# A kernel of attention and two feed-forward layers: four writes and two reads in place of one and five for the transposed coarse probabilities of the later pairs

## The chip, the core and the metric

The kernel runs on one core of a Trainium2 chip. Its five engines each work off their own instructions in order: TensorE (PE in the profile; PEld is its weight load), VectorE (DVE), ScalarE (ACT), GpSimd (POOL) and SyncE (SP), which issues nearly all transfers. The metric is the time of one execution on the device in microseconds, the median over runs.

## What is computed

Attention over 4 batches of 8 heads, 576 positions of 64 numbers, then two feed-forward layers over the 2304 tokens. The attention is the sum of a coarse one, over means of four positions, repeated to full length, and a local one, over a band of three positions to each side. Cut to that:

```python
q_d = q.reshape(B, H, Sd, factor, D).mean(axis=3)      # k_d, v_d alike; Sd = 144
out_d = sm_attn(q_d, k_d, v_d)                         # softmax(q_d k_d' / 8) v_d
out_up = np.repeat(out_d, factor, axis=2)
mask = np.abs(pos[:, None] - pos[None, :]) < factor
scores = np.where(mask, scale * np.matmul(q, k.transpose(0, 1, 3, 2)), -1000000000.0)
out_local = np.matmul(softmax(scores), v)
x = (out_up + out_local)                               # to [2304, 512]
x = _moe_ref(x, w_in, w_out)                           # h = x @ w_in; h * sigmoid(1.702 h) @ w_out
return _moe2_ref(x, w2_in, w2_out)                     # h = x @ w_in; max(0.01 h, h) @ w_out
```

## The kernel before

A pair is two heads of one batch: 16 pairs, numbered 0 to 15 in the order in which they are worked on (`Job` objects, the index into `jobs`). Pairs 0 to 7 are interleaved by a table of tokens, `ORDER`. Pairs 8 to 15, the later pairs, run beside the first feed-forward layer: its loop over blocks of tokens and slices of the hidden layer (`units`) calls `l1_part` (line 860), `gate` and `l2` (line 901), and each unit has two places in which steps of a later pair may stand (`turns`). `Job.slots` is the table of these steps: its keys are the places, counted from the pair's start, and its strings name the steps in the order in which they are issued. A new pair starts every six places.

All engines follow the order in which the program is written (a manual schedule). So on SP the transfers of a later pair stand in one line with those of the feed-forward layers: loads of weights `s` (line 168), writes of converted weights `wsf` (line 232), rows of the attention's result `xd` (line 745), and each is issued when its turn has come and its waits are over. Transfers signal on eight semaphores used in turn; one that takes a semaphore waits until the transfer eight before it has landed.

The steps of a later pair that matter here, with the names in the profile:

- `Mud` scales the coarse probabilities `pd` (128 rows of 3 x 160 numbers, line 539); `Bd` transposes them in blocks of 32 x 32 on DVE (line 588) into a second `pd` tile; `Bds` writes that to DRAM, tensor `tdd` (line 596); `Bdl` reads `tdd` back into `pdT` (line 602) so that the key positions lie on the partitions: 96 rows and 48 rows.
- `Bl` transposes the local probabilities `P` in blocks (line 662), `Bls` writes them to DRAM, tensor `td`, in four writes (line 671), `Bll` reads them back as `pT` (line 674).
- `vh` loads the values for the local attention in two transfers (line 398). `Va0`, `Va1`, `Vb0`, `Vb1` sum the values by fours on POOL (line 440).
- `Vd` multiplies `pdT` by the summed values on PE (`avd`, line 632) and `Y` multiplies `pT` by `vh` (`av_halves`, line 700), right behind it; both stand at place 13 or 14, between units of the feed-forward layer.

After the later pairs come the rest of the first layer and the second layer, to the end of the span; PE works through them in order.

Of the kernel before, what the change touches and what calls it, by code (L numbers as in the profile page):

```python
# [7 lines left out]
F32 = mybir.dt.float32  # L8
# [8 lines left out]
P = 128  # L17
# [6 lines left out]
DK = (96, 48)  # L24
# [3 lines left out]
def attn_moe_kernel(ctx: ExitStack, tc, qT_d, kT_d, vh_d, vg_d, w1a, w2a, w1b, w2b, outT):  # L28
    nc = tc.nc
# [6 lines left out]
    SD = S // FACTOR  # L36
# [56 lines left out]
    dram = ctx.enter_context(tc.tile_pool(name="dram", bufs=1, space=bass.MemoryType.DRAM))  # L93
# [11 lines left out]
    def slot(name):  # L105
# [20 lines left out]
        out=ident, in_=ident, compare_op=ALU.not_equal, fill=1.0, base=0,  # L126
# [5 lines left out]
    for r in (slice(0, KT), slice(KT, P)):  # L132
        nc.gpsimd.affine_select(
            out=bands[r], in_=bands[r], compare_op=ALU.is_ge, fill=NEG, base=0,
# [3 lines left out]
            out=bands[r], in_=bands[r], compare_op=ALU.is_ge, fill=NEG, base=2 * HALO,  # L138
# [183 lines left out]
    ND, DS, DN = 3, 40, 48  # L322
    SDP = -(-SD // 32) * 32

    class Job:
# [265 lines left out]
            )  # L591

        def blocks_d_out(self):
            self.td = dram.tile([P, SDP // 32, ND * 32], F32, name=f"tdd_{self.nm}")
            t = self.td_t.rearrange("p t n -> p (t n)").rearrange("p (c n) -> p c n", n=ND * 32)
            nc.sync.dma_start(out=self.td, in_=t)

        def blocks_d_in(self):
            self.pdT = self.tile([DK[0], 2, ND * P], "pdT")
            for c in range(SDP // 32):  # L600
                n = min(32, SD - c * 32)
                nc.sync.dma_start(
                    out=self.pdT[c % 3 * 32 : c % 3 * 32 + n, c // 3, :].rearrange("p (b n) -> p b n", b=4),
                    in_=self.td[:, c].rearrange("(b k) n -> k b n", b=4)[:n],
                )

        def avd(self, tag):
# [169 lines left out]
        def slots(self):  # L777
            names = {
                -2: "q k",
                1: "Qd",  # L780
                3: "S Kd",
                4: "A0 A1 Mx",
                5: "Sb",
                6: "Ex va vb",
                7: "Sd Mxd Exd Sm Rc Mu",
                8: "Rcd Mud Bd Bds Bl Va0 Vb0 vh Bls",
                10: "Bdl Va1 Vb1 Bll",
                14 if self is jobs[-1] else 13: "Vd Y Od X0 X1",
                16: "O",
            }  # L790
            st = self.steps()
            st.update({
                "Bd": self.blocks_d, "Bds": self.blocks_d_out, "Bdl": self.blocks_d_in,
                "Bl": self.blocks, "Bls": self.blocks_out, "Bll": self.blocks_in,
                "Y": lambda: self.av_halves("h"), "X0": lambda: self.out(0), "X1": lambda: self.out(1), "O": self.store,
            })
            return {i: [lambda n=n: self.step(st, n) for n in x.split()] for i, x in names.items()}
# [454 lines left out]
    with tc.manual_schedule(engines={ET.PE, ET.DVE, ET.Pool, ET.Activation, ET.SP}):  # L1252
# [32 lines left out]
        for u in range(UNITS, len(units)):  # L1285
# [25 lines left out]
            else:  # L1311
# [3 lines left out]
                if m in XSUM:  # L1315
                    a = XSUM.index(m) * 8 // len(XSUM)
# [61 lines left out]
```

## Time and profile before

| | us |
|---|---|
| median of 3 runs | 852.65 (852.0 to 852.66) |
| the profiled execution | 853.28 |
| its span on the core | 851.5 |
| around the span | 1.78 |
| PE busy in the span | 839.5 |
| granted TensorE clock, share of full | 0.998 |
| DMA issued by SP | 203.95 MB in 76800 packets |

The span runs from the first to the last instruction. A row of a timeline names the start in the span and the duration, the engine (SPq and PEq are the sequencers of SP and PE, where waits and issues stand), the line of the kernel, the operation, and the tiles as out<-in, with the count of instructions merged into the row; what stands in brackets is idle time before it and what ended it. A line of the kernel is L596 and so on. The duration of a transfer's row on SP is the time that its issue takes on SP, not the time until the data are there; that is the landing time.

### The profile page before, as it was taken

The page shows a single profiled execution, that of the slowest core. Times are in us where ns is not written, and L with a number is a line of the kernel's source. Part 1 is how long each engine was busy: PE and PEld are TensorE (multiplying, and loading weights), DVE is VectorE, ACT ScalarE, POOL GpSimd, SP SyncE. Part 2 cuts the span into 40 slices and gives each one's busy share as a digit, 9 for nine tenths or more (in the row PEclk, how much of TensorE's full clock was granted, in tenths as well). Part 3 has the DMA queues.
Part 4 walks back from the last instruction along what each step waited for, and adds up shares of the span by engine and source line. Part 5 has one row for each costly group of instructions (what it writes and reads, how often), then busy time and mean ns, then how long its engine had stood idle before and what let it go on. Part 6 is the DMA issues. An engine that isn't in the chain of part 4 may idle for free.

```text
span 851.5 us, 15694 instructions
## 1 busy us (share of the span) xinstructions
PE 839.5 (99%) x5736; PEld 762.6 (90%) x5736; DVE 539.5 (63%) x950; ACT 405.5 (48%) x972; POOL 475.2 (56%) x470
## 2 busy tenths in 40 slices
PE   8899999999999999999999999999999999999998
PEld 5677878887887788899999999999999999999998
DVE  6877776655567543467655757468564767573565
ACT  6876554433334332555655534455434454334460
POOL 6554433745446443777746833459554577455574
PEclk9999999999999999999999999999999999999999
DMA  9755545375765642989949978977779877787654
GB/s 292 250 161 183 183 144 157 116 238 170 196 191 144 221 132 101 341 335 420 370 150 324 343 268 277 334 248 259 265 257 353 286 235 271 267 287 266 221 190 181
DMA packets 76877, 204.95 MB, mean 241 GB/s; under 512 B 14656, under 2 KB 30016, under 8 KB 70400
## 3 DMA queue, kind: packets, MB, share of 16 engines
q1 hardware_dynamic: 76800, 203.95, 70.8%
q8 instruction: 45, 0.74, 0.4%
q14 instruction: 32, 0.26, 0.1%
HBM read 155.42 MB, written 48.50 MB: 239 GB/s over the span
## 4 chain that ended last, share of the span: by engine, by line
PE 92%; DVE 3%; ACT 1%; DMA 1%; issue 1%; SPq 1%; POOL 0%; DVEq 0%; POOLq 0%; ACTq 0%
PE h L860 23%; PE acc L901 22%; PE p L1107 21%; PE h L1032 21%; PE avd L632 1%; PE scd L549 1%; PE sc L455 1%; PE av L684 1%; DMA s<-w1a 1%; PE idle L1225 1%; ACT a L510 1%; PE av L700 0%; DMA pT<-td 0%; PE pt L651 0%; DVE s L188 0%
## 5 line engine op out<-in xcount | busy, mean ns | idle before, releaser
L1086 POOL TENSOR_TENSOR ring<-raw,ring 128x384 fp32r<-128x384 f32 x148 | 166.5, 1136 | 144.3 <-ACT ring L1084 142.8
L860 PE MATMUL h<-xh,w 128*128 128x512 f32 (+1 forms) x640 | 198.6, 373 | 0.0
L1107 PE MATMUL p<-ring,v 128*128 128x384 f32 x900 | 178.9, 334 | 0.0
L901 PE MATMUL acc<-gh,w 128*128 128x512 f32 (+1 forms) x560 | 173.2, 372 | 0.0
L1107 PEld LDWEIGHTS p<-ring,v 128*128 128x128 f32 x900 | 158.1, 188 | 0.1
L1032 PE MATMUL h<-x,v 128*128 128x384 f32 x672 | 137.4, 334 | 0.0
L860 PEld LDWEIGHTS h<-xh,w 128*128 128x128 f32 x640 | 119.1, 188 | 17.3 <-issue 1.4
L886 POOL TENSOR_TENSOR gl<-g,gh 128x512 fp32r<-128x512 f32 (+1 forms) x59 | 71.8, 1216 | 97.2 <-ACT gh L159 96.5
L1032 PEld LDWEIGHTS h<-x,v 128*128 128x128 f32 x672 | 118.4, 188 | 0.0
L860 PE MATMUL h<-xl,w 128*128 128x512 f32 (+1 forms) x320 | 117.9, 368 | 0.0
L901 PEld LDWEIGHTS acc<-gh,w 128*128 128x128 f32 x560 | 104.1, 188 | 14.8 <-issue 0.4
L901 PE MATMUL acc<-gl,w 128*128 128x512 f32 (+1 forms) x280 | 103.7, 370 | 0.0
L880 DVE SCALAR_TENSOR_TENSOR g<-g,h 128x512 f32<-128x512 f32 (+1 forms) x80 | 50.4, 630 | 79.1 <-ACT g L879 78.6
L879 ACT ACTIVATE g<-h 128x512 f32<-128x512 f32 (+1 forms) x80 | 44.0, 550 | 100.5 <-PE h L860 96.7
L1039 ACT ACTIVATE raw<-raw 128x384 f32<-128x384 f32 x72 | 37.9, 526 | 109.1 <-DVE raw L1042 108.9
L1072 DVE TENSOR_TENSOR raw<-raw,raw 128x384 f32<-128x384 f32 x84 | 76.7, 946 | 15.1 <-ACT raw L1039 13.0
L1042 DVE TENSOR_TENSOR raw<-h,u 128x384 f32<-128x384 f32 x72 | 40.1, 557 | 72.1 <-PE h L1032 71.6
L1084 ACT ACTIVATE ring<-raw 128x384 fp32r<-128x384 f32 x150 | 73.5, 515 | 0.0
L1032 PE MATMUL h<-x_ra,v 128*128 128x384 f32 x336 | 72.5, 334 | 0.0
L159 ACT ACTIVATE gh<-g 128x512 fp32r<-128x512 f32 (+1 forms) x70 | 41.7, 595 | 62.7 <-DVE g L880 58.8
L860 PEld LDWEIGHTS h<-xl,w 128*128 128x128 f32 x320 | 60.4, 189 | 6.9
L211 POOL TENSOR_TENSOR w<-t,w 128x512 fp32r<-128x512 f32 x25 | 33.1, 1327 | 48.5 <-ACT w L159 42.2
(188 smaller groups left out, 1271.3 us busy)
## 6 DMA issues: line engine op xcount, KB each, us to landing
v<-ws SPq DMA_DIRECT2D x42, 1024.0 KB, 6.5
v<-ws SPq DMA_DIRECT2D x72, 512.0 KB, 4.6
ws<-wo SPq DMA_DIRECT2D x16, 1792.0 KB, 10.3
s<-w1a SPq DMA_DIRECT2D x16, 512.0 KB, 4.6
s<-w2a SPq DMA_DIRECT2D x16, 512.0 KB, 4.6
s<-w1b SPq DMA_DIRECT2D x16, 512.0 KB, 5.8
s<-w2b SPq DMA_DIRECT2D x16, 512.0 KB, 9.4
v<-ws SPq DMA_DIRECT2D x24, 256.0 KB, 4.4
```

The lines of the kernel that those rows point to most:

```text
L159: return nc.scalar.activation(out=out, in_=in_, func=AF.Copy, scale=scale)
L860: nc.tensor.matmul(h, w[:, kc * P : (kc + 1) * P], xs[kc][part], start=kc == 0 and i == 0, stop=kc == KC - 1 and i == 2,)
L879: lambda: nc.scalar.activation(out=g, in_=h[:, :n], func=AF.Tanh, scale=0.5 * 1.702),
L880: lambda: nc.vector.scalar_tensor_tensor(out=g, in0=g, scalar=1.0, in1=h[:, :n], op0=ALU.add, op1=ALU.mult),
L886: lambda: on(G).tensor_tensor(out=gl, in0=g, in1=gh.bitcast(F32), op=ALU.subtract),
L901: nc.tensor.matmul(acc[c][:, :n], w[:, cs], g, start=m == 0 and i == 0, stop=m == NM - 1 and i == 2)
L1032: nc.tensor.matmul(h, w[:, a, ks], x, start=not more and kt == 0 and k == 0, stop=kt == 1 and k == 2, skip_group_check=True,)
L1042: nc.vector.tensor_tensor(out=out, in0=h, in1=u, op=ALU.add)
L1072: nc.vector.tensor_tensor(out=o, in0=a, in1=b, op=ALU.subtract)
L1084: nc.scalar.activation(out=hi, in_=t, func=AF.Copy)
L1086: e.tensor_tensor(out=lo, in0=t, in1=hi.bitcast(F32), op=ALU.subtract)
L1107: nc.tensor.matmul(self.bank[pair, ct][:, :N2], w[:, q, a, cs], g, start=not more and q == 0 and k == 0, stop=q == QC - 1 and k == 2, skip ...
```

## The change

Three things, for pairs 8 to 15 alone:

- the tensor `tdd` in DRAM is laid out with the key position outermost, [160, 4, 96] in place of [128, 5, 96]. It is written in four transfers of 32 partitions each, every partition as five pieces of 96 numbers (384 bytes), in place of one transfer of 128 partitions with 1920 bytes each;
- `pdT` is read in two transfers, 96 and 48 partitions with one piece of 1536 bytes each, in place of five of 32 (the last 16) partitions with four pieces of 384 bytes each;
- in the table of places `Bls` stands ahead of `Va0 Vb0 vh`, and `Bll` ahead of `Va1 Vb1`.

```diff
         def blocks_d_out(self):
-            self.td = dram.tile([P, SDP // 32, ND * 32], F32, name=f"tdd_{self.nm}")
-            t = self.td_t.rearrange("p t n -> p (t n)").rearrange("p (c n) -> p c n", n=ND * 32)
-            nc.sync.dma_start(out=self.td, in_=t)
+            self.td = dram.tile([SDP, 4, ND * 32], F32, name=f"tdd_{self.nm}")
+            td = self.td.rearrange("(c k) b n -> b k c n", k=32)
+            for b in range(4):
+                t = self.td_t[b * 32 : (b + 1) * 32].rearrange("p t n -> p (t n)")
+                nc.sync.dma_start(out=td[b], in_=t.rearrange("p (c n) -> p c n", n=ND * 32))
 
         def blocks_d_in(self):
             self.pdT = self.tile([DK[0], 2, ND * P], "pdT")
-            for c in range(SDP // 32):
-                n = min(32, SD - c * 32)
+            for kh, a in enumerate((0, DK[0])):
                 nc.sync.dma_start(
-                    out=self.pdT[c % 3 * 32 : c % 3 * 32 + n, c // 3, :].rearrange("p (b n) -> p b n", b=4),
-                    in_=self.td[:, c].rearrange("(b k) n -> k b n", b=4)[:n],
+                    out=self.pdT[: DK[kh], kh, :], in_=self.td[a : a + DK[kh]].rearrange("p b n -> p (b n)")
                 )
...
-                8: "Rcd Mud Bd Bds Bl Va0 Vb0 vh Bls",
-                10: "Bdl Va1 Vb1 Bll",
+                8: "Rcd Mud Bd Bds Bl Bls Va0 Vb0 vh",
+                10: "Bdl Bll Va1 Vb1",
```

The engines PE, DVE, ACT and POOL have the same instructions in the same order in both kernels; only SP's line differs, and the waits that PE makes. On SP, the transfers of pair 13 (the numbers in the names count tiles; 32x5x96 is partitions by pieces by numbers, x4 is four in a row):

```order
-L596 DMA tdd_1_3368<-pd_1_16_3366 128x480
-L398 DMA vh_1_18_3374<-vh 64x2x320 x2
-L671 DMA td_1_3377<-P_1_17_3370 32x2x320 x4
-L232 DMA wsf_104<-t_3_0_3144 128x512
+L598 DMA tdd_1_3368<-pd_1_16_3366 32x5x96 x4
+L671 DMA td_1_3375<-P_1_17_3373 32x2x320 x4
+L398 DMA vh_1_18_3382<-vh 64x2x320 x2
+L232 DMA wsf_104<-t_3_0_3147 128x512
 L745 DMA xd_0_93<-x_0_23_3302 128x576
-L602 DMA pdT_1_19_3440<-tdd_1_3368 32x4x96 x4
-L602 DMA pdT_1_19_3440<-tdd_1_3368 16x4x96
-L674 DMA pT_1_5_2970<-td_1_3377 128x640
+L603 DMA pdT_1_19_3443<-tdd_1_3368 96x384
+L603 DMA pdT_1_19_3443<-tdd_1_3368 48x384
+L674 DMA pT_1_5_2970<-td_1_3375 128x640
```

The writes of `tdd` are four, those of `td` have moved ahead of the loads of `vh`, and three reads of `pdT` are gone; from the first write up to the read of `pT` there are 14 transfers before and after. On PE, at the products of the same pair, the waits before (each name in brackets is one semaphore; DMAHW0 to 7 are those of the transfers):

```order
1430 L632 MATMUL avd_1_20_3535<-pdT_1_19_3440,vd_1_3_2968 64x160 [waits DMAHW4_49,DMAHW3_49,DMAHW5_49,DVE_49,Pool_49]
1431 L632 MATMUL avd_1_20_3535<-pdT_1_19_3440,vd_1_3_2968 64x160
1432 L632 MATMUL avd_1_20_3535<-pdT_1_19_3440,vd_1_3_2968 64x160 [waits DMAHW7_49,DMAHW6_49,Pool_49]
1434 L700 MATMUL avd_1_20_3535<-pT_1_5_2970,vh_1_18_3374 64x64 [waits DMAHW0_49]
1435 L700 MATMUL av_1_21_3540<-pT_1_5_2970,vh_1_18_3374 64x64
```

and now:

```order
1430 L632 MATMUL avd_1_20_3535<-pdT_1_19_3443,vd_1_3_2968 64x160 [waits DMAHW6_49,DVE_49,Pool_49]
1431 L632 MATMUL avd_1_20_3535<-pdT_1_19_3443,vd_1_3_2968 64x160
1432 L632 MATMUL avd_1_20_3535<-pdT_1_19_3443,vd_1_3_2968 64x160 [waits DMAHW7_49,Pool_49]
1434 L700 MATMUL avd_1_20_3535<-pT_1_5_2970,vh_1_18_3382 64x64 [waits DMAHW2_49,DMAHW0_49]
1435 L700 MATMUL av_1_21_3540<-pT_1_5_2970,vh_1_18_3382 64x64 [waits DMAHW3_49]
```

The products on `pdT` wait for one transfer each in place of three and two; the first two products on `pT` wait for the two loads of `vh` by name.

## Rows read from the trace of the kernel before

**Rows 1.** The page's busy times: engine, us, share of the span, instructions.

```profile
PE 839.5 (99%) x5736; PEld 762.6 (90%) x5736; DVE 539.5 (63%) x950; ACT 405.5 (48%) x972; POOL 475.2 (56%) x470
```

**Rows 2.** Who waited for whom: us in total, times, longest.

```profile
PE avd L700 <- DMA pT<-td: 1.3, 1, 1.3
PE avd L632 <- DMA pdT<-tdd: 0.7, 1, 0.7
```

**Rows 3.** Timeline of PE, pair 13: start us, us, what, [idle before].

```profile
270.65 0.39 PE L901 MATMUL acc<-gh,w 128*128 128x512 f32 x1
271.71 1.09 PE L632 MATMUL avd<-pdT,vd 96*64 96x160 f32 x8 [0.68 <-DMA pdT<-tdd]
274.11 0.27 PE L700 MATMUL avd<-pT,vh 64*64 64x64 f32 x1 [1.31 <-DMA pT<-td]
```

**Rows 4.** Timeline of SP, pair 13: start us, us, issues.

```profile
263.00 0.34 SPq L596 DMA_DIRECT2D tdd<-pd  x1
263.44 1.77 SPq L398 DMA_DIRECT2D vh<-vh  x2
265.31 1.96 SPq L671 DMA_DIRECT2D td<-P  x4
267.31 0.42 SPq L232 DMA_DIRECT2D wsf<-t  x1
267.77 0.45 SPq L745 DMA_DIRECT2D xd<-x  x1
268.27 2.43 SPq L602 DMA_DIRECT2D pdT<-tdd  x5
270.74 0.43 SPq L674 DMA_DIRECT2D pT<-td  x1
```

**Rows 5.** DMA issues by line: KB each, median us from issue to landing.

```profile
vh<-vh SPq DMA_DIRECT2D x16, 160.0 KB, 3.1
pT<-td SPq DMA_DIRECT2D x8, 320.0 KB, 3.3
tdd<-pd SPq DMA_DIRECT2D x8, 240.0 KB, 2.1
xd<-x SPq DMA_DIRECT2D x4, 32.0 KB, 2.6
```

**Rows 6.** Single source lines: ns min/median/max of an issue, first and last start.

```profile
L596 SPq DMA_DIRECT2D tdd<-pd x8: 319/336/345, 161.2 to 302.9; - x8
L671 SPq DMA_DIRECT2D td<-P x32: 303/426/937, 163.1 to 306.3; - x32
L398 SPq DMA_DIRECT2D vh<-vh x16: 597/607/1365, 161.6 to 304.0; - x16
L602 SPq DMA_DIRECT2D pdT<-tdd x40: 429/432/511, 166.0 to 309.8; - x40
```

**Rows 7.** Timeline of DVE, pair 13: the transpose that td is written from.

```profile
262.90 0.80 DVE L662 STREAM_TRANSPOSE P<-P 128x640 f32<-128x640 f32 x1
```

**Rows 8.** DMA issues of 243 to 248 us (pair 12), then of 268 to 271.

```profile
pT<-td SPq DMA_DIRECT2D x1, 320.0 KB, 3.2
pdT<-tdd SPq DMA_DIRECT2D x4, 48.0 KB, 3.5
...
pdT<-tdd SPq DMA_DIRECT2D x4, 48.0 KB, 2.3
```

**Rows 9.** Line 632: PE's separate waits, ns min/median/max.

```profile
L632 PEldq EVENT_SEMAPHORE  x36: 51/51/642, 36.3 to 313.4; - x36
```

**Rows 10.** Timeline, pairs 10 and 11: the issue of pT and PE's first product on it.

```profile
209.07 0.42 SPq L674 DMA_DIRECT2D pT<-td  x1
...
212.49 0.28 PE L700 MATMUL av<-pT,vh 64*64 64x64 f32 x2
...
228.18 0.42 SPq L674 DMA_DIRECT2D pT<-td  x1
...
232.07 0.34 PE L700 MATMUL av<-pT,vh 64*64 64x64 f32 x4
```

## The prediction

> **What bounds the kernel now.** The page's busy times come first: PE is busy for 839.5 us of a span of 851.5 us [rows 1], 99%. A change that leaves every matmul where it is can only act through the 12 us in which PE has nothing to do, and this one touches eight places of them, the two blocks of value products (lines 632 and 700) of each later pair, numbered 8 to 15 here. So the second view is the list of who waited for whom, read for PE waiting on the transfers that the change rewrites. It has one wait on pdT and one on pT, each a single time [rows 2]: seven of the eight pairs show none. The third view, PE's timeline, says where: pair 13. The last matmul of line 901 starts at 270.65, the products on pdT at 271.71 after 0.68 us of idle time, those on pT at 274.11 after 1.31 us more [rows 3]. Without the waits they would start at about 270.65 + 0.39 and go on at once, and the eight take 1.09 us with the wait between them, so the stretch from 271.04 to 274.11 holds some 2.0 to 2.7 us of stall: the most that any shortening of this path could give back, 0.3% of the time.
>
> The fourth view, SP's timeline, says why pT comes late there. SP issues one transfer after another without a pause from 263.00 to 270.74: the write of tdd, two loads of vh, four writes of td, wsf, xd, five reads of pdT, then the read of pT [rows 4]. pT is not late because its data are late; it stands in line behind 14 others. From its issue to PE's start are 274.11 - 270.74 = 3.37 us, which is the usual landing time of pT, 3.3 us [rows 5]. The step that decides is therefore **when SP's turn comes to pT**, and the change must be counted in SP's issue slots.
>
> **The change, part by part.** *Four writes for one.* Three issues are added ahead of pT. The trace has no write of 32 rows by 5 pieces; the nearest is the write of td, 32 partitions by 2 pieces from the same kind of tile: 426 ns in the median [rows 6], and four take 2.00 us with the gaps between them (265.31 to 267.31 [rows 4]), 0.50 each. The reads of pdT, which also walk 32 rows by 4 pieces of 384 bytes, take 432 ns, five in 2.47 us, 0.49 each. I take 0.49: +1.47 us. Bounds: a plain 128-row write takes 319 ns at best, a load of vh 607 ns in the median [rows 6]; over the four writes that is 4 x (0.319 - 0.426) = -0.43 and 4 x (0.607 - 0.426) = +0.72 us about the value taken.
>
> *Two reads for five.* Three issues go: 3 x 0.49 = -1.47 us. The two that stay are a row of 1536 bytes per partition and take what the read of pT takes, 0.43 [rows 4].
>
> *The loads of vh behind the writes of td.* The same six issues in another order: 0 us for pT, which stands behind both. The writes of td need the DVE transpose, done at 262.90 + 0.80 = 263.70 [rows 7]; the four writes of tdd keep SP busy until 263.00 + 0.44 + 3 x 0.49 = 264.91, so no wait appears. vh would go out at 266.9 and about 267.9, later than now by some 3.4 us, and land 3.1 us on [rows 5], by 271.0; PE wants it with pT at 274.1. Cover 3 us, and in the other pairs it is issued at least two slots before pT and lands sooner than pT does. The reads of pT and the pooling of v swap places in the text only: they are on different engines.
>
> Pair 13 anew: 263.00 + 0.44 + 1.47 (tdd) + 2.00 (td) + 1.87 (vh) + 0.46 (wsf) + 0.50 (xd) = 269.74, two reads of pdT to 270.72, pT issued at **270.72 instead of 270.74**. The sum is three more and three fewer of the same thing on the same queue: 0.0 us.
>
> *What lands later?* pdT's reads now start 1.5 us later, at 269.74 and 270.23. Their landing: 2.3 us for the narrow reads in this stretch, 3.5 where a load of 512 KB goes ahead [rows 8], 3.3 for the larger pT: 272.0 to 273.7, before pT's 274.0. PE then starts its pdT products later but still ends them before pT is there; the stall moves from one label to the other and keeps its end. Where a weight load goes ahead, the same bytes drain in the same order, and fewer pieces do not make them slower.
>
> *The queue's bytes.* Ahead of wsf and xd now stand 320 KB of td (4 x 80), then 320 KB of vh: the same load in front of pdT and pT. The 512 KB ahead of pair 12's reads put 1.2 us on pdT, and nothing on pT: 3.2 us [rows 8].
>
> *PE's own waits.* Per pair the first product on pdT waits for three things instead of five and the second for two instead of three, while the first product on pT gains a wait and its neighbour another, since vh is no longer covered by an earlier wait. A separate wait takes 51 ns [rows 9]; one less and one more is 0, with bounds of 8 x 0.051 = 0.4 us either way.
>
> *The writes' landing.* SP may issue the reads of pdT only when all four writes of tdd have landed. The last goes out at 264.4, the first read at 269.74: 5.3 us of room. The write lands in 2.1 us now, and the writes of xd with 256 bytes per row (32 KB over 128 partitions), the nearest thing to pieces of 384 bytes, in 2.6 [rows 5]. Hidden, with 2.7 us to spare.
> The Trainium skill ("DMA: Bandwidth & Descriptors", section Specifications) speaks against the change here: under 512 bytes a transfer is read, modified and written, and line rate is lost. The 0.5 us between 2.6 and 2.1 agrees in sign. By it the new writes would be the slow kind, and the sum would still be 0.0 as long as they land within the room; what comes if they do not is the second rival.
>
> **The sum.** Profiled execution 853.28 us (span 851.5 and 1.78 around it), change 0.0: 853.3. The median of the runs is 852.65, 0.63 below the profiled one, so the forecast for the median is **852.6**. A difference of under 0.2% (1.7 us) is about what a measurement of this kernel cannot tell from no change.
>
> **Rivals.** *The issue of the new writes is dearer.* If five pieces per row cost what vh's issue costs, pT goes out 0.72 us later in every pair. Pair 13 pays 0.72. Pair 10 has no slack: pT issued at 209.07 lands at 212.4, PE starts on it at 212.49 [rows 10]; it pays 0.65. Pair 11: 228.18 + 3.3 = 231.5 against 232.07, slack 0.6, pays 0.15. Together +1.5: 854.1, still within 0.2%. For it: vh's 607 ns are not explained by its count of pieces, 64 x 2, which is that of a read of pdT, 32 x 4. Against: td's writes, the closest shape, are at 426. Chance 0.10.
>
> *Slower: small writes land late.* The reads of pdT on SP then wait for tdd, and pT, q, kT and the weight loads are queued behind that wait. It decides from a landing time of 5.3 us in pair 13; at 7 us the wait is 1.7 there, up to 1.7 in pair 10 and 1.1 in pair 11: +4.5, 857.1. Against: no small write in the views is near it (2.1 and 2.6 in the median). Chance 0.06.
>
> *Faster: the stall of pair 13 goes.* The writes of td start 0.4 us sooner (264.91 against 265.31), and the two loads of vh took 1.77 us there against 2 x (0.607 + 0.05) = 1.31 by the median: one issue was stretched by 0.46. If such stretches belong to the transfer and not to the moment, pT goes out 0.5 sooner; with cheap writes 0.9. To reach 0.2% more than half the stall would have to go, by a read of pT that is also 0.8 us quicker once 576 small pieces no longer run ahead of it: 852.65 - 2.0 = 850.6. Against: 512 KB ahead of it do not move its 3.2 us. Chance 0.07.
>
> *It does nothing that can be seen,* because every move is inside one queue's line: that is the forecast, 0.77 for it.
>
> **How the numbers follow.** The range takes the bounds of the costs: below, -0.43 (cheap writes) - 0.46 (the stretch gone) - 0.4 (PE's waits) = -1.3; above, +1.5 (dear writes) + 0.3 of another stretch in pair 13 or 10 = +1.8. So 851.3 to 854.4, which leaves out most of the second and third rival, 0.13, and some of the tails. Faster by over 0.2%: 0.07; slower: 0.06 from the late landing and 0.03 from dear writes with a stretch on top, 0.09; within: 0.84.
>
> **What would show it.** In the profile after: in pair 13 SP's line runs from the first write of tdd to pT in 7.7 us, as now, with four issues of about 0.43 at its head and two before pT; PE starts on pT within 0.5 us of 274.1 on the span's clock; the list of waits still has pT as PE's one wait on a transfer of these, a little longer, and pdT's shorter or longer by what pT's changes the other way. Wrong would be: a wait of SP at line 603 (the second rival), issues of line 598 near 0.6 (the first), no wait on pT at all (the third), or a wait on vh at line 700 (then the cover of 3 us was misread).

## The result, and the profile after

The changed kernel takes **857.99 us** (854.79 to 862.09, 8 runs) against 852.65 (851.54 to 853.54, 8 runs) for the one before: 1.0063 times as long, with a 95% interval of 1.0040 to 1.0087. The forecast was 852.6, no change, with a range up to 854.4. A later comparison (2 runs of the changed kernel) gave 857.92 against 852.43, 1.0068 (1.0048 to 1.0088). So the change makes the kernel about 5.4 us slower, and the prediction of no change was wrong: the time lies 3.6 us above the upper end of its range.

The profiled execution took 860.19 us, its span is 858.4. The page's busy times answer [rows 1]:

```profile
PE 841.5 (98%) x5736; PEld 763.7 (89%) x5736; DVE 538.5 (63%) x950; ACT 405.2 (47%) x972; POOL 475.7 (55%) x470
```

PE is busy 2.0 us longer with the same 5736 matmuls, and idle for 16.9 us instead of 12.0. Part of the first is chance: in this one execution the granted clock is 0.50 from 51.8 to 55.2 us, ahead of the later pairs, where it is 1.00 in the kernel before and in the second profile of the changed kernel (below). The list of waits names the idle time (us in total, times, longest; against [rows 2]):

```profile
PE avd L632 <- DMA pdT<-tdd: 5.1, 5, 3.4
PEld avd L700 <- DMA pT<-td: 0.9, 3, 0.3
```

Before, PE waited for pdT once, 0.7 us; now five times, 5.1 us. The longest is in pair 13, on PE's timeline (start, duration, [idle before]; against [rows 3]):

```profile
275.97 0.39 PE L901 MATMUL acc<-gh,w 128*128 128x512 f32 x1
279.75 0.49 PE L632 MATMUL avd<-pdT,vd 96*64 96x160 f32 x4 [3.40 <-DMA pdT<-tdd]
280.63 0.80 PE L632 MATMUL avd<-pdT,vd 48*64 48x160 f32 x4 [0.39 <-DMA pdT<-tdd]
281.27 0.36 PE L700 MATMUL avd<-pT,vh 64*64 64x64 f32 x1
```

From the last matmul of line 901 to the products on pT are 5.30 us; in [rows 3] it was 3.46. SP's timeline for the same pair, against [rows 4]:

```profile
268.66 2.53 SPq L598 DMA_DIRECT2D tdd<-pd  x4
271.29 1.82 SPq L671 DMA_DIRECT2D td<-P  x4
273.21 1.25 SPq L398 DMA_DIRECT2D vh<-vh  x2
274.51 0.59 SPq L232 DMA_DIRECT2D wsf<-t  x1
275.16 0.42 SPq L745 DMA_DIRECT2D xd<-x  x1
275.62 1.12 SPq L603 DMA_DIRECT2D pdT<-tdd  x2
276.85 0.37 SPq L674 DMA_DIRECT2D pT<-td  x1
```

The line is the one that was forecast: pT is issued at 276.85, 8.19 us behind the first write (before 7.74, forecast 7.7; one of the four writes was stretched to 1.18 us). What differs is the time from issue to landing (KB each, median us; all transfers of the stretch in which the later pairs run; against [rows 5] and the 2.3 and 3.5 us of [rows 8]):

```profile
vh<-vh SPq DMA_DIRECT2D x16, 160.0 KB, 3.0
pT<-td SPq DMA_DIRECT2D x8, 320.0 KB, 4.7
tdd<-pd SPq DMA_DIRECT2D x32, 60.0 KB, 1.8
pdT<-tdd SPq DMA_DIRECT2D x8, 144.0 KB, 4.5
pdT<-tdd SPq DMA_DIRECT2D x8, 72.0 KB, 4.3
```

The new writes land sooner than the old one, 1.8 us against 2.1, vh as before, but **pT lands in 4.7 us instead of 3.3 and pdT in about 4.4**. The transfer rates point to the reason. Two rows of the busy times by stretch, first of before, then of after, from the first write of tdd to the issue of pT in pair 13 (the last two columns are the DMA engines' busy share and GB/s):

```profile
263.00:270.70 7.70, 7.70 (x36) 6.33 (x34) 6.76 (x12) 2.77 (x5) 6.10 (x9) 1.00 0.71 207
```

```profile
268.70:276.80 8.10, 7.66 (x34) 6.01 (x32) 7.18 (x13) 3.13 (x7) 6.53 (x8) 1.00 0.55 142
```

The same 14 transfers are issued in these stretches. Before, the DMA engines move 207 x 7.7 = 1.59 MB in the time; after, 142 x 8.1 = 1.15 MB, although it is 0.4 us longer (in the second profile of the changed kernel, without a stretched write, 153 x 7.2 = 1.10 MB). SP is busy all the time, but with small transfers first: eight issues for 560 KB, and only then 1.1 MB in six issues. When pT is issued, some 0.44 MB more than before are still to be moved.

### The profile page after: what moved, and what is told of

Read it like the earlier page. It is cut to its first block, busy times and chain, and to the rows that moved or that the text cites. A ratio compares the mean times of both kernels' runs of the same rounds, so it can differ in the third digit from the quotient of the medians.

```text
span 858.4 us, 15704 instructions
## 1 busy us (share of the span) xinstructions
PE 841.5 (98%) x5736; PEld 763.7 (89%) x5736; DVE 538.5 (63%) x950; ACT 405.2 (47%) x972; POOL 475.7 (55%) x470
## 4 chain that ended last, share of the span: by engine, by line
PE 90%; DMA 5%; SPq 1%; DVE 1%; ACT 1%; issue 0%; DVEq 0%; ACTq 0%
PE h L860 22%; PE acc L901 21%; PE p L1107 20%; PE h L1032 20%; DMA pdT<-tdd 2%; DMA kT<-kT 1%; PE sc L455 1%; PE avd L632 1%; PE scd L549 1%; PE av L684 1%; DMA s<-w2a 1%; DMA a<-qT 1%; DMA a<-vg 1%; PE avd L700 0%; PE pt L651 0%
```

## Where the time went, in one table

For each of the eight pairs four moments were read off, all counted from the first write of tdd: the issue of the first bulk transfer behind tdd, td and vh (wsf, a weight load or xd, 256 to 512 KB), the issue of pT, its landing, and the length of the block, which is the time from the start of PE's last product before line 632 to that of its first after line 700. A block without a wait takes 1.58 us (pair 15: 1.74). In pair 13 before: bulk 267.31 - 263.00 = 4.31, pT issued 7.74, there 11.06, block 4.11. The table has the means over the pairs and the sum of the blocks, one profile each, and the ratio of the times. The labels are those of the experiments below.

| kernel | bulk issued | pT issued | pT there | bulk to pT there | sum of blocks | time / before |
|---|---|---|---|---|---|---|
| before | 4.06 | 7.50 | 10.77 | 6.70 | 15.4 | 1 |
| after | 5.69 | 7.71 | 12.24 | 6.55 | 20.7 | 1.0063 |
| after, again | 5.62 | 7.62 | 12.26 | 6.64 | 21.1 | 1.0068 |
| e1_layout | 5.95 | 7.89 | 12.00 | 6.04 | 17.9 | 1.0046 |
| e2_order | 4.17 | 7.69 | 11.08 | 6.91 | 15.3 | 1.0008 |
| e3_v_first | 4.21 | 6.33 | 10.49 | 6.28 | 14.6 | 0.9999 |
| e4_v_first_old | 2.91 | 6.50 | 9.83 | 6.92 | 14.2 | 0.9974 |
| e5_four_five | 5.82 | 9.02 | 12.29 | 6.46 | 21.5 | 1.0085 |
| e6_split | 5.70 | 8.96 | 12.41 | 6.70 | 20.8 | 1.0086 |
| e7_reads_early | none | 6.94 | 11.10 | | 17.6 | 1.0021 |
| e8_best | none | 5.69 | 8.92 | | 13.3 | 0.9967 |
| e9_both | none | 5.78 | 8.98 | | 13.7 | 0.9973 |

The blocks account for the loss in size: 20.7 - 15.4 = 5.3 us, and the medians differ by 857.99 - 852.65 = 5.3. That the two agree so closely is luck, since blocks come from one execution and medians from several: the spans of the two profiled executions differ by 858.4 - 851.5 = 6.9 us, and in the second profile of the changed kernel the blocks add 5.8 us and the span 4.7. Pair 13 pays 2.3 of it (4.11 to 6.42); pairs 8 to 11, which had no wait before, pay 0.3 to 1.2 each.

## The experiments

Two theories came first. **Q**: the order of SP's queue is to blame; vh's 320 KB now stand right ahead of the bulk transfers and the reads, whatever the size of the pieces. **L**: the layout is to blame; small pieces are slow to write or wide rows slow to read.

**Layout alone** (the four writes and two reads of the change, the table of places of before):

```diff
-                8: "Rcd Mud Bd Bds Bl Bls Va0 Vb0 vh",
-                10: "Bdl Bll Va1 Vb1",
+                8: "Rcd Mud Bd Bds Bl Va0 Vb0 vh Bls",
+                10: "Bdl Va1 Vb1 Bll",
```

(against the changed kernel). 

> The new layout alone (four writes of tdd, two reads of pdT), with the table of places of before, so that the loads of vh stand ahead of the writes of td. Theory Q (the queue): after the change 320 KB of vh, 256 KB of wsf and up to 288 KB of xd are issued within 2.4 us right ahead of the reads, and the reads wait in the queue behind these bytes; the pieces' size does not matter. Then, with vh early again, pT lands 3.3 to 3.9 us after its issue (median; before 3.3, changed kernel 4.7), pdT 3 to 3.8, and the time is 852 to 854.5 us. Theory L (the layout: pieces of 384 bytes written, rows of 1536 bytes read): the landings stay at 4.4 and more, and the time at 856 to 859.

Measured 855.91 against 852.48, 1.0046 (1.0027 to 1.0065): between the ranges of Q (up to 854.5) and L (from 856). So are the landings:

```profile
pT<-td SPq DMA_DIRECT2D x8, 320.0 KB, 4.1
pdT<-tdd SPq DMA_DIRECT2D x8, 144.0 KB, 3.5
pdT<-tdd SPq DMA_DIRECT2D x8, 72.0 KB, 3.3
```

**Order alone** (the layout, write and reads of before, the table of places of the change):

```diff
-                8: "Rcd Mud Bd Bds Bl Va0 Vb0 vh Bls",
-                10: "Bdl Va1 Vb1 Bll",
+                8: "Rcd Mud Bd Bds Bl Bls Va0 Vb0 vh",
+                10: "Bdl Bll Va1 Vb1",
```

> The new table of places alone (the writes of td ahead of the loads of vh), with the old layout (one write, five reads). Theory Q: vh's bytes now go out after those of td, close ahead of the reads, but the five reads of pdT give the queue 2.4 us to drain before pT is issued: pdT lands later than before (3 to 4.5 us instead of 2.8), pT in 3.3 to 4.2, the time is 853 to 856 us. Theory L: nothing moves, 852 to 853.5 us, landings as before.

Measured 853.23, 1.0008 (0.9995 to 1.0022): no difference that can be seen (the value lies in both forecasts). So most of the loss comes with the layout, and Q as stated falls. But the landings of e1_layout do not suit L either. In pair 13 pT lands in 3.4 us, about as before, and in four pairs in 4.4 to 5.3; the median is 4.1. The wide rows are those of pdT: the first read of each pair lands in 2.5 to 2.9 us in pairs 9, 10, 13 and 14, where wsf or xd goes ahead of it, and in 4.2 to 5.1 in pairs 8, 11, 12 and 15, where a weight load of 512 KB does. The narrow reads of before show the same split, 2.1 to 2.5 and 3.9 to 4.6 us. So the shape of the wide rows is not what makes them slow.

**vh ahead of everything**, with the layout of the change, then with that of before:

```diff
-                8: "Rcd Mud Bd Bds Bl Bls Va0 Vb0 vh",
+                8: "vh Rcd Mud Bd Bds Bl Bls Va0 Vb0",
```

> The changed kernel with the two loads of vh moved to the head of place 8, ahead of the steps that SP waits for, where SP stands idle before; nothing else differs. Theory Q: the 320 KB are gone from the line, pT is issued about 6.5 us after the first write of tdd instead of 8.2 and lands 3.2 to 3.9 us later; PE waits on pT or pdT at most once, by under 2 us; 850 to 852.5 us. Theory L: the landings stay at 4.4 us and more and the time stays above 854.

> The kernel of before with the loads of vh at the head of place 8 (and the writes of td right behind that of tdd); old layout, one write and five reads. Theory Q: pT is issued about 6.4 us after the write of tdd instead of 7.7, lands in 3.3 us, the stall of pair 13 shrinks by about 1.3 us: 850.5 to 852 us, the same as the new layout with vh first within 0.5 us. Theory L: as fast as that or faster, while the new layout with vh first stays slow.

Measured 851.58, 0.9999 (0.9984 to 1.0014), and 850.55, 0.9974 (0.9965 to 0.9984). The second beats the kernel before. Of the two theories' forecasts for e3_v_first, Q has the time (850 to 852.5) and L the landing (pT in 4.6 us in the median). vh out of the way gains 6.4 us on the changed kernel and 1.9 on the one before, since bulk and pT are issued 1.0 to 1.5 us sooner; what is left between the two, 1.0 us by the medians and 2.1 by the ratios, is the layout's. The table shows a later arrival: in e3_v_first pT is issued even 0.17 us sooner than in e4_v_first_old (6.33 against 6.50) and is there 0.66 us later (10.49 against 9.83), while the bulk starts 1.30 us later (4.21 against 2.91). It does not explain the time, though: pT is 0.8 to 1.5 us later in the four pairs behind a weight load, which have slack for it here, and in pair 13 no later; the blocks add 0.4 us.

That gave a third theory, **S**: what decides is when the bulk is issued. Three issues moved from behind the bulk to ahead of it put the bulk off, and pT, which must wait for the bulk's bytes, comes later by as much; the three issues saved behind the bulk give back little.

**Four writes, but five reads** (rows of 1536 bytes, 32 partitions at a time; places as before):

```diff
-            for kh, a in enumerate((0, DK[0])):
+            for c in range(SDP // 32):
+                n = min(32, SD - c * 32)
                 nc.sync.dma_start(
-                    out=self.pdT[: DK[kh], kh, :], in_=self.td[a : a + DK[kh]].rearrange("p b n -> p (b n)")
+                    out=self.pdT[c % 3 * 32 : c % 3 * 32 + n, c // 3, :],
+                    in_=self.td[c * 32 : c * 32 + n].rearrange("p b n -> p (b n)"),
```

> The new layout with four writes of 32x5x96, but read in five transfers (32 or 16 partitions, one piece of 1536 bytes each); table of places as before. Theory S (what costs is the issue slots moved ahead of the bulk transfers: whatever is added ahead of wsf, xd or the weight load makes these and then pT later, and slots saved behind them give nothing): three slots are added and none is saved, pT is issued 1.4 us later than before, about 9.2 us after the first write in pair 13, lands in 3.0 to 3.5 us after that because the five reads stand between the bulk and it; 855.5 to 857.5 us. Rival L (wide rows are slow to read, or small pieces slow to write, by themselves): pT and pdT land in 4.4 us or more as well, on top of the later issue; 858 us or more.

Measured 859.86 against 852.19, 1.0085 (1.0072 to 1.0099), 2.4 us above the upper end of what was expected. The landings are what S says (issues and landings of the stretch of the later pairs):

```profile
pT<-td SPq DMA_DIRECT2D x8, 320.0 KB, 3.2
pdT<-tdd SPq DMA_DIRECT2D x32, 48.0 KB, 3.0
```

The same wide rows, read out of the same layout, land about as fast as the narrow ones did before (3.0 us against 2.8). Yet pT is not there any sooner than in the changed kernel: 12.29 us after the first write, against 12.24. It is issued 1.3 us later and lands 1.3 us faster. Against e1_layout, from which it differs by its number of reads alone, the three reads more cost 1.13 us of issue (9.02 against 7.89) and 0.29 us of arrival (12.29 against 12.00). So three slots behind the bulk are worth a quarter of themselves in the mean. They are not worth nothing, though: in pair 13 they are worth 1.27 us (12.85 against 11.58), and the times differ by 0.4%. The mean hides a split: behind a weight load (pairs 8, 11, 12, 15) pT comes 0.1 us sooner with five reads than with two, in the other four pairs 0.7 later, and pairs 10 and 13, which have no slack, are among these.

**Four writes of the old kind**: no small pieces, no wide rows, nothing but three more issues.

```diff
-            nc.sync.dma_start(out=self.td, in_=t)
+            for b in range(4):
+                nc.sync.dma_start(out=self.td[b * 32 : (b + 1) * 32], in_=t[b * 32 : (b + 1) * 32])
```

> Layout, reads and table of places of before; only the one write of tdd is cut into four of 32 partitions, 1920 bytes each. No small piece is written, no wide row is read. Theory S: three slots are added ahead of the bulk transfers, pT goes out 1.0 to 1.4 us later; its landing stays at 3.0 to 3.5 us; 855 to 857 us. Rival L: nothing of its two causes is here, only three issue slots: pT 1.0 to 1.4 us later costs only what the slack of pairs 13, 10 and 11 does not cover, 853.5 to 855 us.

Measured 859.89, 1.0086 (1.0069 to 1.0103), again 2.9 us above S's upper end, and no different from e5_four_five with its small pieces and wide rows. **So L falls: neither small pieces nor wide rows are needed for a loss of this size; three issue slots ahead of the bulk are enough.** Here no slot is saved behind the bulk, so pT itself goes out 1.46 us later than before (8.96 against 7.50); that the loss does not need this rests on the changed kernel, where it goes out 0.2 us later, on its second profile below, and on e1_layout against e5_four_five. The landings of this kernel, and SP's timeline in pair 13:

```profile
pT<-td SPq DMA_DIRECT2D x8, 320.0 KB, 3.3
tdd<-pd SPq DMA_DIRECT2D x32, 60.0 KB, 1.7
```

```profile
266.68 2.48 SPq L597 DMA_DIRECT2D tdd<-pd  x4
...
272.61 0.42 SPq L232 DMA_DIRECT2D wsf<-t  x1
...
273.56 2.43 SPq L603 DMA_DIRECT2D pdT<-tdd  x5
276.04 0.43 SPq L675 DMA_DIRECT2D pT<-td  x1
```

wsf goes out 5.93 us after the first write instead of 4.31, and pT is there 3.16 us after its issue, at 279.20: 6.59 us after wsf. Before, that stretch was 274.06 - 267.31 = 6.75, in e5_four_five 6.61, in the changed kernel 281.23 - 274.51 = 6.72, with pT issued 3.4 us behind wsf in three of them and 2.3 in the last.

How much each side counts can be estimated from the kept traces: nine of the twelve profiles have a bulk transfer ahead of the reads, which makes 72 arrivals of pT, and a least-squares fit gives each pair a constant and each of the two delays a weight. Behind a weight load (pairs 8, 11, 12, 15) the arrival moves by 0.95 us for each us of the bulk's issue and by 0.10 for each us of pT's own. Behind wsf or xd (pairs 9, 10, 13, 14) it moves by 0.46 and 0.42, all four give or take 0.1. So S holds as it stands for the first four pairs; in the others, pair 13 with the longest stall among them, pT's own turn counts about as much as the bulk's.

Of the 2 to 3 us that S had missed, a part is the clock. In the profiles of these two kernels the granted clock is at its lower level, 1.2 of 2.4 GHz, for 6.8 us behind the stall of pair 13, twice as long as before; 3.4 us more at half speed are up to 1.7 us. The row for e6_split (PEclk is the third figure from the right):

```profile
276.90:283.70 6.80, 5.91 (x64) 4.27 (x65) 2.52 (x9) 1.31 (x8) 0.00 (x0) 0.50 0.87 253
```

**The reads ahead of the bulk**, in the layout of the change:

```diff
-                8: "Rcd Mud Bd Bds Bl Bls Va0 Vb0 vh",
-                10: "Bdl Bll Va1 Vb1",
+                8: "Rcd Mud Bd Bds Bl Bls vh Bdl Bll Va0 Vb0",
+                10: "Va1 Vb1",
```

> The changed kernel with the two reads of pdT and the read of pT at the end of place 8, right behind the loads of vh and ahead of wsf, the weight loads and xd (in pair 13: tdd x4, td x4, vh x2, pdT x2, pT, then the bulk). Theory S: nothing of the bulk is ahead of pT any more, it is issued 6.6 to 7.5 us after the first write and lands in 3 to 3.5 us, PE does not wait for it in any pair but perhaps 13; 849.5 to 852 us. Rival L: the rows and pieces are slow wherever they stand: landings of pdT and pT of 4.4 us or more in the median, and 852 us or more.

Measured 854.66, 1.0021 (1.0009 to 1.0033). That is 3.3 us better than the changed kernel and above what S had expected (849.5 to 852). L's time came (852 or more), its landings of 4.4 us or more did not: 4.0 us for pT, 3.1 and 3.2 for the reads of pdT. SP's timeline shows vh in the place that the bulk had:

```profile
270.04 1.55 SPq L398 DMA_DIRECT2D vh<-vh  x2
271.71 0.99 SPq L603 DMA_DIRECT2D pdT<-tdd  x2
272.87 0.34 SPq L674 DMA_DIRECT2D pT<-td  x1
273.26 0.42 SPq L232 DMA_DIRECT2D wsf<-t  x1
```

The three reads are issued right behind the 320 KB of vh, and pT lands in 4.0 us in the median, 3.85 here. What is large and right ahead of the reads need not be wsf or a weight load.

**Neither bulk nor vh ahead of the reads**, first in the layout of before, then in that of the change:

```diff
-                8: "Rcd Mud Bd Bds Bl Va0 Vb0 vh Bls",
-                10: "Bdl Va1 Vb1 Bll",
+                8: "vh Rcd Mud Bd Bds Bl Bls Bdl Bll Va0 Vb0",
+                10: "Va1 Vb1",
```

> Layout, one write and five reads of before; vh at the head of place 8, then tdd, td, and the reads of pdT and pT at its end, ahead of the bulk transfers. pT is issued some 5 us after the write of tdd. Theory S: lands in about 3 us, so no wait of PE on pdT or pT in any pair, also pair 13; all eight blocks at 1.6 us; 849 to 850.5 us, no slower than the kernel with vh first alone (850.55). Rival L says the same of this kernel, since neither small pieces nor wide rows are in it; it shows how much of the stalls there is to get.

> Layout, four writes and two reads of the changed kernel, but in the order of e8_best: vh at the head of place 8, the reads of pdT and pT at its end, ahead of wsf, the weight loads and xd. Theory S': pT is there some 6.6 us after the first bulk transfer ahead of it in the queue has been issued (6.70 in the mean of the eight pairs before, 6.55 after, 6.46 and 6.70 with five reads, 6.04 with the layout alone), however many reads stand between; four small writes cost only because they put this transfer off. Here no bulk is between, so pT is issued 5 to 6.2 us after the first write, lands in 3 to 3.6 us, no pair but 13 waits, and that one under 1 us: 849.3 to 851, within 0.1% of e8_best (849.68). Rival: small writes or wide rows have a price of their own that e8_best does not pay; then pT is there 1 us later or more than in e8_best (8.9 us after the first write in the mean), pair 13 waits about 1.5 us and more: 851.5 to 853.

Measured 849.68, 0.9967 (0.9954 to 0.9979), and 850.24, 0.9973 (0.9962 to 0.9984). Both beat the kernel before, and they cannot be told apart: four small writes and two wide reads cost nothing that can be seen where nothing large is in the queue right ahead of the reads. In e8_best pair 13 still waits 0.23 us for pT, where no wait was expected. The landings of the second, and its PE at pair 13:

```profile
pT<-td SPq DMA_DIRECT2D x8, 320.0 KB, 3.2
tdd<-pd SPq DMA_DIRECT2D x32, 60.0 KB, 1.8
pdT<-tdd SPq DMA_DIRECT2D x8, 144.0 KB, 2.3
pdT<-tdd SPq DMA_DIRECT2D x8, 72.0 KB, 2.2
```

```profile
270.95 0.39 PE L901 MATMUL acc<-gh,w 128*128 128x512 f32 x1
271.27 0.91 PE L632 MATMUL avd<-pdT,vd 96*64 96x160 f32 x8
272.77 0.24 PE L700 MATMUL avd<-pT,vh 64*64 64x64 f32 x1 [0.58 <-DMA pT<-td]
```

The same transfers of 144 and 72 KB land in 2.3 and 2.2 us here, in 4.5 and 4.3 in the changed kernel. The other seven pairs have no wait.

**The changed kernel again**, for one more profile.

> The changed kernel once more. In its first profile the first write of tdd comes at 163.71 us, in the kernel before at 161.24, although nothing of the change stands ahead of it. If that is chance, it comes anywhere from 161 to 163.7 here; the eight blocks of value products take 19 to 22 us again, pT comes 12.0 to 12.4 us after the first write in the mean, and the clock falls behind pair 13: 855 to 860 us.

Measured 857.92. The first write of tdd comes at 161.06 us, so the 2.5 us by which the first profile was late ahead of the change were chance (its lower clock at 51.8 us is a part of them). And here no write of tdd is stretched in pair 13 (SP's timeline, then the landing of the pT issued right behind it):

```profile
267.22 1.80 SPq L598 DMA_DIRECT2D tdd<-pd  x4
...
273.45 0.92 SPq L603 DMA_DIRECT2D pdT<-tdd  x2
274.48 0.37 SPq L674 DMA_DIRECT2D pT<-td  x1
```

```profile
pT<-td SPq DMA_DIRECT2D x1, 320.0 KB, 4.5
```

pT is issued 7.26 us after the first write, 0.48 *sooner* than before, and is there 0.73 later: 11.79 against 11.06. The count of issue slots was right, and by itself it did not decide.

## Why the prediction was wrong, point by point

- *Four writes for one, two reads for five.* Right in the median. The issue of a new write takes 436 ns, that of a new read 435; forecast 0.43 to 0.49. The mean of the writes is 511 ns, since a few are stretched (last section), which puts the bulk off by 1.63 us where 1.47 were added in the sum. The mean issue of pT moved by 0.2 us (7.50 to 7.71), forecast 0.0. The row of the new line, which answers line 596 in [rows 6]:

```profile
L598 SPq DMA_DIRECT2D tdd<-pd x32: 322/436/1772, 163.7 to 311.1; - x32
```

- *The writes' landing.* Right, and better than the bound: 1.8 us, no wait of SP on line 603. The rule of the Trainium skill ("DMA: Bandwidth & Descriptors", Specifications) on pieces under 512 bytes, that weighed against the change, does not show in the landings: pieces of 384 bytes land in 1.8 us, the same 60 KB in rows of 1920 bytes (e6_split) in 1.7.
- *The loads of vh.* Right as to their own cover: they land in 3.0 us and PE never waits for them. Wrong as to what they do to others: they were counted as issues, and their 320 KB had come to stand right ahead of the bulk. Order alone costs nothing that can be seen (e2_order), but with the layout it seems to add: the stretch from bulk to pT is 6.04 in e1_layout and 6.55 after, and the blocks are 17.9 and 20.7, while the intervals of the two times overlap (1.0027 to 1.0065, 1.0040 to 1.0087). In pair 13 it is 278.64 - 273.11 = 5.53 against 6.72, most of the way from the block of 4.60 there to 6.42.
- ***What lands later?* and *The queue's bytes*: the steps that failed.** The landing of pT was taken as a constant, 3.3 us, that of pdT as 2.3 to 3.5. Measured: 4.7 and 4.3 to 4.5. The sentence "the same bytes drain in the same order, and fewer pieces do not make them slower" is contradicted by no run, and misses that the bytes begin to drain 1.6 us later. "The same load in front of pdT and pT" counts the bytes; it leaves out how long they have had to drain when pT joins the queue, 3.4 us before and 2.0 after in the mean. The row that seemed to speak for it, 512 KB ahead of pair 12's reads and 3.2 us for pT all the same [rows 8], had the five reads' 2.4 us between the two.
- *The sum.* pT's arrival was taken as its issue plus 3.3 us. The runs fit better with the issue of the bulk plus some 6.0 to 6.9 us, alone or together with pT's own issue (the fit above). A single trace cannot show this: before, 7.50 + 3.26 and 4.06 + 6.70 are two ways to write the same arrival, so only the first was seen. The three added issues moved the second by 1.6 us, and the three removed ones only the first. Had the sum been made for the bulk's issue as well, [rows 4] would have given it: wsf at 267.31 + 1.47, pT at 274.06 + 1.47 = 275.5, and 1.47 us less slack in each pair. The slack from pT's landing to PE's first product on it is, in the trace of before, 1.37, 0.91, 0.05, 0.80 and 1.47 us in pairs 8 to 12, 0.04 in pair 13 and over 2 in 14 and 15; so the estimate would have been 0.10 + 0.56 + 1.42 + 0.67 + 0.00 + 1.43 = +4.2 us, where +5.3 was measured.
- *PE's own waits.* No effect could be seen in the blocks without a stall, 1.58 us both times.
- *Rivals.* None of the three happened. "Small writes land late" had the right size, +4.5 us by pairs 13, 10 and 11, but by luck: its mechanism is refuted by the landing of 1.8 us. The list of what would show the prediction wrong had no entry for a later landing of the reads.

## What to carry to other kernels

On a queue that mixes small and large transfers, an issue slot is worth something different on each side of the bulk: ahead of it, a slot delays the bulk and all that follows; behind it, a slot costs less, and saving it gains less. In this kernel it was worth about a tenth of itself behind a weight load of 512 KB and some four tenths behind wsf or xd (the estimate above). So count two times for each transfer that is waited for, its turn at the issuing engine and its turn among the bytes, and take landing times as results of the queue, not as properties of the transfer. Put the reads that an engine waits for ahead of the bulk, and what can be loaded early (here vh) earlier still: with that, 849.68 us, 0.3% below the kernel before, and the layout no longer shows in the time.

## What was not expected of the hardware

- *The clock can make a stall cost twice.* In the kernel before, the granted clock behind the stall of pair 13 falls to the lower level:

```profile
275.00:278.20 3.20, 3.20 (x18) 2.47 (x14) 2.62 (x9) 1.41 (x8) 0.00 (x0) 0.51 0.92 267
```

  At that level (1.2 of 2.4 GHz) the twelve products of line 549 start over 1.21 us, and over 0.68 us in the next pair at full clock. Behind pair 13 the changed kernel has the same once, e5_four_five and e6_split for 6.8 us, e8_best and e9_both, with stalls of 0.23 and 0.58 us, not at all:

```profile
270.50:277.00 6.50, 5.92 (x76) 4.40 (x75) 4.63 (x13) 4.03 (x14) 1.45 (x3) 1.00 0.95 311
```

  So an idle time of PE can cost more than itself, and the gain of e8_best over before has two parts, 2.0 us of blocks and up to 1.7 of clock (half of the 3.4 us at the lower level). The length of the stall alone does not decide: e1_layout keeps the full clock at pair 13 with a block of 4.60 us, the kernel before does not with 4.11. What decides was not tried.
- *An issue on SP is stretched now and then.* Four of the 32 writes of line 598 took 0.68 to 1.77 us where the median is 0.44, and in before two loads of vh 1.12 and 1.37 us where the median is 0.61 [rows 6]. It makes single profiles differ by a microsecond at one pair. It is not all chance: in all eight profiles with four writes one write of pair 8 takes 1.25 to 1.83 us and one of pair 11 0.94 to 1.56, while the single write of before never takes more than 0.35. Why was not tried.
- *What stays open.* Why bulk and reads together take 6.0 to 6.9 us was not resolved into bytes and latencies, nor why pT's own turn counts behind wsf and xd and hardly behind a weight load: single pairs lie between 4.9 and 8.2 us, and a weight load of 512 KB by itself is no slower than wsf and xd together (6.11 in pair 8, 6.76 in pair 13, both before).
